# Seven products in two batches instead of five, staging in the plain ones, and W13's stores issued later

## The chip, the core and the metric

The kernel runs on one core of a Trainium2 chip. The metric is the device time of one execution in microseconds; below it is the median of three executions. The engines are TensorE (PE, its weight loads PEld), VectorE (DVE), ScalarE (ACT), GpSimd (POOL) and SyncE (SP), which here only issues DMAs. Each engine takes its instructions in the order of its own queue.

## What is computed

Attention over a packed key set, then two feed-forward blocks, all in float32:

```python
p_packed = sm_attn(p, k, v)               # 8 batches, 8 heads, 32 packed rows, head_dim 64
x = sm_attn(q, p_packed, p_packed)        # 576 rows a batch and head
x = x.transpose(0, 2, 1, 3).reshape(4608, 512)
x2 = (((x @ w1) * (x @ w2)) @ w3) @ w_out     # 512 -> 1024 -> 1024 -> 512
h = x2 @ w_in                                 # 512 -> 2048
out = np.maximum(0.01 * h, h) @ moe2_w_out    # 2048 -> 512
```

## The kernel before

**Numbers.** A float32 operand is used as two parts, hi (rounded) and lo (the remainder), and a product is three matmuls (hi.hi, hi.lo, lo.hi). hi is made on Scalar by a copy, lo on Vector by a subtraction (the helper `sub`, L154). The weights come as 64-bit words; each piece is converted on Scalar (`word`, L293), Vector (`bits`, L299 and L302) and GpSimd (`join`, L309).

**Phase one** goes over eight batches of 576 tokens. `w3 @ w_out` is one matrix, W13, held in four tiles (tags `wr` and `ws`). For a batch there are AT (the second softmax, two tiles) and M (the packed rows times w1 and w2, four tiles); `ab_mm` multiplies them into 16 units of 12 matmuls (a and b for one of 8 feature chunks and one of two token halves of 288), and a times b is the operand of x2. In a *plain* batch (`pieces`, L507) each unit's product is split into hi and lo, and eight units of 24 matmuls make x2 (`x2_unit`). In a batch with *seven products* (`pieces_s`, L776) a times b is kept raw (`ab_raw`), sums of quarters are formed (`x_sum`, L716), each of the seven operands is split (`x_form`, L722 and L154), and seven products of 24 matmuls (`x_product`, L738) take the place of the eight units. The seven matching forms of W13 are made once, in batch 1, from the four quarters (`w13_form`: raw sums on GpSimd, L669; hi and lo), stored to `w13f`, and streamed back in every seven-product batch (`w13_load`). `w13_out` stores W13 itself, to `w13d` (four stores of 1 MB) and, for three of the quarters, to `w13f` (twelve of 256 KB); `w13_back` loads it again for batch 7, which is plain.

**Beside them.** While batch b's pieces run, the attention of batch b+1 is worked in (`attention` in plain batches, `attention_s` in the others): k, q, v loads, scores (`s1_mm`, `s2_mm`), two softmaxes, M's first pair. `pump` and `conv_flush` convert the second block's weights piece by piece. `stage_att(u, a)` stages x2 for phase two: it loads four quarters of 384 columns of one half, forms seven operands (`FORM_B`: 4 sums, 7 hi, 7 lo) and stores them to `xfd`. It borrows the attention's buffers: raw quarters in `v` (5), lo in `PT` (2), hi in `P` (2). One half is staged in each of batches 2 to 6; one more (`stage_b(2, 1)`) in batch 7, the rest in phase two.

**Phase two** (L1013, from 581 us) multiplies the staged operands with forms of w_in and w_out2, also by seven products.

**What sets the order.** The pieces of a batch are numbered slots, 0 to 15 for the units of `ab_mm`, 16 on for x2; tables give the slot at which each further step is written (`slots`, L511). A scheduler then orders each engine's queue by readiness and that order of writing. The prologue and batch 0 have their order written out by hand in `SCRIPT`, on all engines but SP, whose loads and stores the scheduler places. `after(ins, other)` adds an order, not a wait of its own.

Of the kernel before, what the change touches and what calls it, by code (L numbers as in the profile page):

```python
# [55 lines left out]
def tile_kernel(ctx, tc, qT, kT, vL, pT, w12, w3b, wo1, win, wo2, out):  # L56
# [8 lines left out]
    w13d = dram.tile([4, P, 2, 2, 512], F32, name="w13d")  # L65
    w13f = dram.tile([7, P, 2, 2, 512], F32, name="w13f")
# [347 lines left out]
    abh = {}  # L414
    Mp, Mt, abp, ab32, abt, x2p = {}, {}, {}, {}, {}, {}
# [65 lines left out]
    def x2_store(b, th, e):  # L481
        t = main.tile([P, TH], F32, tag="x2s", name="x2s", bufs=6)
        nc.scalar.copy(t, x2p.pop((b, th, e))[:, :TH])  # L483
        nc.scalar.dma_start(out=x2d[:, e, b * S + th * TH:b * S + (th + 1) * TH], in_=t)
# [33 lines left out]
    def attention_s(b):  # L518
        d = {s: [] for s in range(24)}
        d[0] += [lambda: load_v(b, 0)]  # L520
        d[1] += [lambda: load_v(b, 1)]
        d[1] += [lambda: s1_mm(b)]
        for g in range(2):
            d[1] += [lambda g=g: s1_max(b, g)]
            d[2] += [lambda g=g: s1_exp(b, g)]
            d[3] += [lambda g=g: s1_norm(b, g)]
            d[3 + g] += [lambda g=g: load_kq("q", b, g)]
            d[6] += [lambda g=g: t_mm(b, g)]
        for g in range(2):
            d[6] += [lambda g=g: t_copy(b, g)]  # L530
            d[8] += [lambda g=g: pv_mm(b, g)]
        for g in range(2):
            d[8] += [lambda g=g: pv_scale(b, g)]
        d[10] += [lambda: pp_mm(b), lambda: pp_copy(b)]
        d[12] += [lambda: s2_mm(b)]
        for g in range(2):
            s = 12 + 2 * g
# [4 lines left out]
        d[20] += [lambda: m_pair(b, 0)]  # L542
# [3 lines left out]
        return d  # L546

# [67 lines left out]
    def stage(u, a, raw, new, high):  # L615
# [13 lines left out]
        def step(s):  # L629
            form((s,), x, lambda m: high(), lambda m, x: x.bitcast(F32R), lambda m, x: new() if x is None else x, done)  # L630
# [3 lines left out]
    def stage_att(u, a):  # L634
# [4 lines left out]
        return stage(u, a, tile("v", VB), tile("PT", 2), lambda: tile("P", 2)().bitcast(F32R))  # L639
# [7 lines left out]
    def w13_out():  # L647
        for f in range(4):
            nc.sync.dma_start(out=w13d[f], in_=rd(W13[f]))
        for q, m in AQ.items():  # L650
            if m != 7:
                for fa in range(2):
                    for l in range(2):
                        c = int(q[0]) * 256
                        nc.sync.dma_start(
                            out=w13f[m - 1, :, fa, l].rearrange("p (c e) -> p c e", c=2),
                            in_=rd(W13[2 * int(q[1]) + fa])[:, :, l, c:c + 256],
                        )

    def w13_form(fa):  # L660
# [39 lines left out]
    def ab_raw(b, fc, th):  # L700
# [10 lines left out]
        nc.vector.tensor_tensor(out=rawt[b, f][:, th, fc % 2], in0=pb[:, :TH], in1=a, op=ALU.mult)  # L711
# [13 lines left out]
    def x_product(b, m):  # L725
# [18 lines left out]
        for mb in range(2):  # L744
            def new(i, j, tag="x2s", bufs=6):
                t = dsts[b, i, j, mb] = main.tile([P, TH], F32, tag=tag, name="x2s", bufs=bufs)
                nc.scalar.copy(t, ps[mb])

            def add(i, j):
                t = dsts[b, i, j, mb]  # L750
                nc.vector.tensor_tensor(out=t, in0=ps[mb], in1=t, op=ALU.add)
# [27 lines left out]
    def forms_s(b):  # L779
# [6 lines left out]
            14: [lambda: x_sum(b, 6, 5, 3, 5), ],  # L786
            16: [lambda: x_form(b, 6, 0), lambda: x_form(b, 6, 1), lambda: x_sum(b, 7, 7, 3, 7)],
# [19 lines left out]
    FIRST_S, LAST_S = 2, 6  # L807
# [43 lines left out]
    PUMPS = (0, 6, 6, 6, 5, 5, 4)  # L851
    STAGE = {2: (0, 0), 3: (0, 1), 4: (1, 0), 5: (1, 1), 6: (2, 0)}
    for b in range(1, 7):
        staging = {}
        plain = b < FIRST_S
        if plain:
            w13_out()
            staging = spread(w13_form(0) + w13_form(1), 12, 23)
        elif b in STAGE:
            steps = stage_att(*STAGE[b])  # L860
            staging = spread(steps[1:], 11, 19)
            staging[9] = steps[:1]
# [71 lines left out]
    slots(last, fill, spread(stage_b(2, 1), 17, 23))  # L934
# [245 lines left out]
```

## Time and profile before

| | |
|---|---|
| median of three executions | 1293.17 us (1290.62 to 1294.09) |
| profiled execution, its own time | 1288.82 us |
| span from its first to its last instruction | 1287.0 us |
| TensorE busy | 1243.0 us (97%), 8864 matmuls |
| Vector, Scalar, GpSimd busy | 938.5, 624.1, 125.3 us |
| mean granted TensorE clock | 0.995 of full speed |
| moved by DMA | 322.96 MB, mean 251 GB/s |

Batch 0's matmuls begin at 81 us, batch 1's at 152.5, batch 2's at 219, batch 7's at 527.6. A busy TensorE isn't TensorE at its peak: where the span of a batch and its busy time are close, the number of matmuls and their pace set the time; where they differ, a wait does. The row of a waiting instruction names in brackets how long its engine stood idle and whose result released it.

### The profile page before, as it was taken

Reading aid. Unit: us, or ns where it says so; the run is one execution under the profiler, and the core shown is the slowest. Engines: PE = TensorE matmul, PEld = TensorE weight load, DVE = VectorE, ACT = ScalarE, POOL = GpSimd, SP = SyncE. Lnnn points to the kernel's source line nnn. Section 1 sums busy time; section 2 is a strip of 40 time slices with the busy share of each in tenths; the row PEclk is TensorE's granted clock in tenths of the full one; section 3 lists DMA queues with packets and bytes.
Section 4 is the critical chain, followed back from the end, with each engine's and each line's share of the span. In section 5 each row is a group of like instructions: output and inputs, shape, how many; then the busy total and the mean of one; then the engine's idle time right before and its main releaser. Section 6 shows DMA issues by size and latency. Waiting matters only on the chain.

```text
span 1287.0 us, 23438 instructions
## 1 busy us (share of the span) xinstructions
PE 1243.0 (97%) x8864; PEld 1157.4 (90%) x8864; DVE 938.5 (73%) x1524; ACT 624.1 (48%) x1123; POOL 125.3 (10%) x144
## 2 busy tenths in 40 slices
PE   7879998999999999999999999999999999999998
PEld 3339987888888889899999999999999999999998
DVE  7767487888888979666868754886566457786667
ACT  4335353555555556455656554654333344453332
POOL 6444032111110201000000000000000000000000
PEclk9999998999999999999999999999999999999999
DMA  9995138997979795938887778266635764598883
GB/s 368 363 357 180 57 116 296 331 324 239 314 247 306 234 305 175 359 120 280 282 317 283 269 268 289 103 241 249 234 129 190 257 217 167 208 355 299 294 291 124
DMA packets 149986, 322.96 MB, mean 251 GB/s; under 512 B 15856, under 2 KB 71152, under 8 KB 145904
## 3 DMA queue, kind: packets, MB, share of 16 engines
q1 hardware_dynamic: 140656, 312.01, 69.1%
q10 hardware_dynamic: 9216, 9.44, 2.1%
q8 instruction: 70, 1.15, 0.4%
q14 instruction: 44, 0.36, 0.1%
HBM read 230.69 MB, written 90.70 MB: 250 GB/s over the span
## 4 chain that ended last, share of the span: by engine, by line
PE 78%; DVE 12%; DMA 7%; issue 2%; ACT 1%; SPq 1%; POOL 0%; ACTq 0%; DVEq 0%; POOLq 0%
PE b L1013 30%; PE mm L149 16%; PE c L1013 15%; PE a L1013 8%; PE mm L738 3%; PE at L183 3%; DMA c<-w 2%; PE mm L402 1%; DVE v L154 1%; DVE cT L302 1%; DVE abf L154 1%; DMA c<-w3b 1%; DVE abr L716 1%; DVE abr L711 1%; DVE sT L265 1%
## 5 line engine op out<-in xcount | busy, mean ns | idle before, releaser
L149 PEld LDWEIGHTS mm<-AT,M 128*128 128x128 f32 x1536 | 209.9, 191 | 38.1 <-issue 10.2
L149 PE MATMUL mm<-AT,M 128*128 128x288 f32 x1536 | 224.5, 302 | 18.1 <-DVE ab L458 6.0
L1013 PE MATMUL b<-xh,wi 128*128 128x384 f32 x768 | 216.5, 335 | 0.0
L1013 PE MATMUL b<-gh,wo 128*128 128x384 f32 x768 | 215.3, 335 | 0.7 <-DVE o L965 0.7
L1013 PEld LDWEIGHTS b<-gh,wo 128*128 128x128 f32 x768 | 140.4, 188 | 1.0 <-DVE o L965 1.0
L1013 PEld LDWEIGHTS b<-xh,wi 128*128 128x128 f32 x768 | 140.5, 188 | 0.0
L1013 PE MATMUL b<-xl,wi 128*128 128x384 f32 x384 | 128.4, 334 | 0.0
L1013 PE MATMUL b<-gl,wo 128*128 128x384 f32 x384 | 128.3, 334 | 0.0
L738 PEld LDWEIGHTS mm<-abf,W 128*128 128x128 f32 x840 | 112.7, 188 | 11.8 <-DVE abr L711 5.0
L738 PE MATMUL mm<-abf,W 128*128 128x288 f32 x840 | 118.1, 297 | 4.4 <-DVE abr L711 3.8
L609 ACT CAST gh<-gr 128x1152 fp32r<-128x1152 f32 (+1 forms) x72 | 75.7, 1054 | 77.1 <-PE b L1013 48.0
L1013 PE MATMUL c<-gh,wo 128*128 128x384 f32 x384 | 106.4, 334 | 0.0
L1013 PE MATMUL c<-xh,wi 128*128 128x384 f32 x384 | 105.2, 334 | 0.0
L154 DVE TENSOR_TENSOR gl<-gr,gh 128x1152 fp32r<-128x1152 f32 (+1 forms) x72 | 88.0, 1222 | 16.8 <-ACT gh L609 16.7
L965 DVE TENSOR_TENSOR o<-b,o 128x384 f32<-128x384 f32 x108 | 59.5, 555 | 34.3 <-PE b L1013 34.0
L149 PEld LDWEIGHTS mm<-ab,W 128*128 128x128 f32 x576 | 76.4, 188 | 5.0 <-ACT x2s L483 1.7
L149 PE MATMUL mm<-ab,W 128*128 128x288 f32 x576 | 78.1, 295 | 1.5 <-DVE ab L154 1.3
L959 ACT ACTIVATE gr<-gr 128x1152 f32<-128x1152 f32 (+1 forms) x54 | 57.2, 1060 | 44.1 <-DVE gr L965 43.9
L609 ACT CAST gh<-gs 128x1152 fp32r<-128x1152 f32 (+1 forms) x54 | 56.9, 1054 | 44.8 <-PE b L1013 26.5
L973 ACT COPY gr<-b 128x384 f32<-128x384 f32 x96 | 45.6, 479 | 64.9 <-PE b L1013 64.7
L452 ACT COPY a<-mm 128x288 f32<-128x288 f32 x128 | 49.9, 399 | 49.5 <-PE mm L149 40.2
L402 PE MATMUL mm<-ab,w 128*128 128x512 f32 x128 | 59.4, 618 | 13.8 <-POOL ab L309 8.7
(128 smaller groups left out, 2288.4 us busy)
## 6 DMA issues: line engine op xcount, KB each, us to landing
xh<-xfd SPq DMA_DIRECT2D x126, 384.0 KB, 5.6
xl<-xfd SPq DMA_DIRECT2D x126, 384.0 KB, 5.3
W<-w13f SPq DMA_DIRECT2D x23, 1024.0 KB, 7.1
part<-o SPq DMA_DIRECT2D x48, 384.0 KB, 2.5
o<-part SPq DMA_DIRECT2D x48, 384.0 KB, 6.5
xfd<-xt SPq DMA_DIRECT2D x49, 192.0 KB, 2.7
xfd<-xr SPq DMA_DIRECT2D x49, 192.0 KB, 2.6
raw<-kT SPq DMA_DIRECT2D x32, 288.0 KB, 4.7
```

The lines of the kernel that those rows point to most:

```text
L149: ins = nc.tensor.matmul(dst, lhs(i), rhs(j), start=first and n == 0, stop=last and n == 2)
L154: return engine.tensor_tensor(out=out, in0=x, in1=rd(hi), op=ALU.subtract)
L183: ins = nc.tensor.matmul(dst(h)[c * 32:c * 32 + 32], lhs[r, c, :], rhs(c)[r], start=True, stop=True)
L265: nc.vector.tensor_tensor(out=t, in0=t, in1=st[:, :, 0:1].to_broadcast([P, 18, 32]), op=ALU.subtract)
L402: nc.tensor.matmul(w13p[fc], words["3", i][:, c:c + P], words["o", jc], start=w13n[fc] == 1, stop=w13n[fc] == 8)
L452: nc.scalar.copy(a, pa[:, :TH])
L609: gate("a", nc.scalar.copy(hi[step], x[step]))
L738: ins = nc.tensor.matmul(ps[mb], w[:, fa, i, at:at + P], t[:, j, c], start=m in (1, 5, 2) and fa + c + n == 0, stop=m in (4, 3, 2) and fa ...
L959: nc.scalar.activation(out=out, in_=x, func=AF.Prelu, alpha=0.01)
L965: evicted.append(nc.vector.tensor_tensor(**args))
L973: nc.scalar.copy(out, ps)
L1013: ins = nc.tensor.matmul(dst, lhs(l), rhs(r), start=first and n == 0, stop=last and n == total - 1, skip_group_check=True)
```

## The change

- **Fewer seven-product batches.** `FIRST_S` goes from 2 to 5: batches 2, 3 and 4 become plain; only 5 and 6 have seven products.
- **Staging.** Batches 2, 3 and 4 stage two halves each, `(u, 0)` loaded in slot 7 and formed in slots 10 to 14, `(u, 1)` in slots 11 and 15 to 19. Batches 5, 6 and 7 stage none. Each staging sum and lo is ordered behind the latest product, remainder or x2 copy (`latest`, `tied`).
- **W13.** Its stores are sixteen of 256 KB, all to `w13f` (eight places now, `w13d` goes), written in slots 3 to 9 of batch 1 and ordered behind the last v load of batch 2; `w13_back` reads these sixteen blocks. The forms of W13 are made in slots 11 to 19 of batch 1 instead of 12 to 23. In batch 5 the five form loads are written in slots 2 to 9, ordered behind the v loads of batch 6.
- **Attention.** All batches use `attention_s`, whose steps come earlier: first scores at slot 0, transposes at 5, p.v at 7, second scores at 10 (before: 1, 7, 10, 16 in plain batches, 1, 6, 8, 12 in the others).
- `PUMPS` is 6, 5, 5, 5, 6, 5 (before 6, 6, 6, 5, 5, 4), and one `x_sum` is made earlier.

```diff
-    w13d = dram.tile([4, P, 2, 2, 512], F32, name="w13d")
-    w13f = dram.tile([7, P, 2, 2, 512], F32, name="w13f")
+    w13f = dram.tile([8, P, 2, 2, 512], F32, name="w13f")
...
+    def tied(ins):
+        return after(ins, latest[0])
...
     def attention_s(b):
         d = {s: [] for s in range(24)}
-        d[0] += [lambda: load_v(b, 0)]
-        d[1] += [lambda: load_v(b, 1)]
-        d[1] += [lambda: s1_mm(b)]
+        d[0] += [lambda: load_v(b, 0), lambda: load_v(b, 1)]
+        d[0] += [lambda: s1_mm(b)]
...
-        d[12] += [lambda: s2_mm(b)]
+        d[T4] += [lambda: s2_mm(b)]
...
+    T1, T2, T3, T4, MP = 5, 7, 9, 10, 20
...
-    def w13_out():
-        for f in range(4):
-            nc.sync.dma_start(out=w13d[f], in_=rd(W13[f]))
...
+    def w13_blocks(move):
+        for q, m in RAW_AT.items():
+            for fa in range(2):
+                for l in range(2):
+                    c = int(q[0]) * 256
+                    w = rd(W13[2 * int(q[1]) + fa])[:, :, l, c:c + 256]
+                    move(w, w13f[m, :, fa, l].rearrange("p (c e) -> p c e", c=2))
+
+    def w13_out(ahead, n):
+        part = []
+        w13_blocks(lambda w, d: part.append((w, d)))
+        for w, d in part[4 * n:4 * n + 4]:
+            after(nc.sync.dma_start(out=d, in_=w), ahead[0])
...
     def w13_back():
         W13[:] = [w13_tile(f) for f in range(4)]
-        for f in range(4):
-            nc.sync.dma_start(out=rd(W13[f]), in_=w13d[f])
+        w13_blocks(lambda w, d: nc.sync.dma_start(out=w, in_=d))
...
         if b == FIRST_S:
-            d[0] += [lambda m=m: w13_load(m) for m in (1, 5, 6, 3, 2)]
+            for k, m in ((2, 1), (3, 5), (5, 6), (7, 3), (9, 2)):
+                d[k] += [lambda m=m: after_load(w13_load(m), b)]
...
-    FIRST_S, LAST_S = 2, 6
+    FIRST_S, LAST_S = 5, 6
...
-    PUMPS = (0, 6, 6, 6, 5, 5, 4)
-    STAGE = {2: (0, 0), 3: (0, 1), 4: (1, 0), 5: (1, 1), 6: (2, 0)}
+    PUMPS = (0, 6, 5, 5, 5, 6, 5)
+    STAGE = {2: ((0, 0), (0, 1)), 3: ((1, 0), (1, 1)), 4: ((2, 0), (2, 1))}
     for b in range(1, 7):
         staging = {}
-        plain = b < FIRST_S
-        if plain:
-            w13_out()
-            staging = spread(w13_form(0) + w13_form(1), 12, 23)
...
+        if b == 1:
+            staging = spread(w13_form(0) + w13_form(1), 11, 19)
+            for n in range(4):
+                staging.setdefault(3 + 2 * n, []).append(lambda n=n: w13_out([vload[2]], n))
+        for (load, first, last), ua in zip(((7, 10, 14), (11, 15, 19)), STAGE.get(b, ())):
+            steps = stage_att(*ua)
+            staging.setdefault(load, []).append(steps[0])
+            for k, f in spread(steps[1:], first, last).items():
+                staging.setdefault(k, []).extend(f)
...
-    slots(last, fill, spread(stage_b(2, 1), 17, 23))
+    slots(last, fill)
```

**SP in batch 0.** `c<-w` are loads of w12's words (512 KB, three buffers), `w13f<-W` and `w13d<-W` W13's stores, `W<-w13f` the load of a form. Before, word for word:

```order
L690 DMA W_2429<-w13f 128x2048
L334 DMA c_627<-w 128x1024
L334 DMA c_677<-w 128x1024
L655 DMA w13f<-W_81 128x2x256 x2
L649 DMA w13d<-W_81 128x2048
L655 DMA w13f<-W_80 128x2x256
L649 DMA w13d<-W_80 128x2048
L655 DMA w13f<-W_80 128x2x256
L334 DMA c_681<-w 128x1024
L655 DMA w13f<-W_81 128x2x256
L655 DMA w13f<-W_80 128x2x256
L334 DMA c_684<-w 128x1024
```

The same loads in the changed kernel, on to q and the last word of w12:

```order
L335 DMA c_626<-w 128x1024
L335 DMA c_676<-w 128x1024
L335 DMA c_680<-w 128x1024
L335 DMA c_683<-w 128x1024
L335 DMA c_729<-w 128x1024
L335 DMA c_753<-w 128x1024
L168 DMA raw<-qT 128x576 x4
L163 DMA pks_84<-pT 128x128
L335 DMA c_873<-w 128x1024
```

No store stands among them any more. The stores come later, behind the v loads and ahead of batch 2's k:

```order
L175 DMA v<-vL 128x512
L176 DMA v<-vL 64x128
L672 DMA w13f<-W_77 128x2x256 x2
L672 DMA w13f<-W_78 128x2x256 x2
L672 DMA w13f<-W_79 128x2x256 x2
L672 DMA w13f<-W_80 128x2x256 x2
L672 DMA w13f<-W_79 128x2x256 x2
L672 DMA w13f<-W_80 128x2x256 x2
L672 DMA w13f<-W_77 128x2x256 x2
L672 DMA w13f<-W_78 128x2x256 x2
L168 DMA raw<-kT 128x576 x4
```

**Vector in batch 3, ahead of the second softmax** (`sT<-at`). Before, `abr<-mm,a` is a raw product of a seven-product batch, `abr<-abr` a sum for it; `PT<-v`, `v<-v,P` and `PT<-PT,P` are one half's staging:

```order
L711 TENSOR_TENSOR abr<-mm,a 128x288
L716 TENSOR_TENSOR abr<-abr 128x576 x2
L711 TENSOR_TENSOR abr<-mm,a 128x288
L299 TENSOR_SCALAR cT<-c_3488 128x512
L605 TENSOR_TENSOR PT<-v 128x384
L302 SCALAR_TENSOR_TENSOR cT<-c_3488,cT 128x512
L711 TENSOR_TENSOR abr<-mm,a 128x288
L154 TENSOR_TENSOR v<-v,P 128x384
L605 TENSOR_TENSOR PT<-v,PT 128x384
L605 TENSOR_TENSOR v<-v 128x384
L711 TENSOR_TENSOR abr<-mm,a 128x288
L154 TENSOR_TENSOR PT<-PT,P 128x384
```

In the changed kernel, `ab_3716<-mm,a` is a plain batch's product and `ab<-ab_3716,ab` its remainder:

```order
L464 TENSOR_TENSOR ab_3716<-mm,a 128x288
L153 TENSOR_TENSOR ab<-ab_3716,ab 128x288
L613 TENSOR_TENSOR PT<-v 128x384
L153 TENSOR_TENSOR v<-v,P 128x384
L613 TENSOR_TENSOR PT<-v,PT 128x384
L263 STREAM_TRANSPOSE sT<-at 128x576 x2
L265 TENSOR_REDUCE st_3741<-sT 128x18
L464 TENSOR_TENSOR ab_3777<-mm,a 128x288
L265 TENSOR_REDUCE st_3827<-sT 128x18
L266 TENSOR_TENSOR sT<-sT,st_3741 128x576
L300 TENSOR_SCALAR cT<-c_3241 128x512
L464 TENSOR_TENSOR ab_3814<-mm,a 128x288
```

The sums of raw products are gone and each product has its remainder behind it; the first half's staging still begins just ahead of the second softmax, which now stands among the last units of `ab_mm`, and the second half's comes behind it.

## Rows read from the trace of the kernel before

**Rows 1.** Stretches: length, busy us of engines (instructions), granted clock, DMA share, GB/s.

```profile
152.50:215.10 62.60, 61.07 (x605) 55.41 (x603) 48.47 (x81) 27.76 (x64) 16.20 (x15) 1.00 0.54 182
...
219.00:284.30 65.30, 60.92 (x579) 54.20 (x579) 57.94 (x100) 35.02 (x70) 11.88 (x15) 0.95 0.93 326
284.30:346.40 62.10, 59.63 (x579) 52.62 (x579) 52.80 (x99) 33.73 (x68) 9.66 (x12) 1.00 0.84 280
346.40:408.06 61.66, 59.61 (x579) 52.63 (x580) 52.72 (x96) 33.05 (x67) 7.90 (x11) 1.00 0.83 276
408.06:468.73 60.67, 59.24 (x580) 52.68 (x580) 52.75 (x96) 33.16 (x68) 7.94 (x11) 1.00 0.83 274
468.73:527.57 58.84, 58.58 (x582) 52.53 (x580) 50.50 (x93) 33.14 (x67) 5.78 (x4) 1.00 0.68 240
527.57:581.20 53.63, 53.16 (x419) 51.37 (x418) 32.02 (x67) 26.38 (x64) 0.00 (x0) 1.00 0.63 210
...
650.00:1287.00 637.00, 632.28 (x3637) 631.13 (x3635) 431.59 (x642) 291.61 (x458) 0.00 (x0) 1.00 0.68 240
```

**Rows 2.** TensorE's timeline: start, us, instruction, count, idle before and releaser.

```profile
63.33 13.97 PE L402 MATMUL mm<-ab,w 128*128 128x512 f32 x32 [3.10 <-DVE W L154]
...
94.07 6.74 PE L149 MATMUL mm<-AT,M 128*128 128x288 f32 x30 [5.57 <-DVE ab L458]
...
218.97 0.85 PE L149 MATMUL mm<-AT,M 128*128 128x288 f32 x2 [3.89 <-ACT M L426]
222.12 4.62 PE L149 MATMUL mm<-AT,M 128*128 128x288 f32 x22 [2.29 <-DVE M L154]
...
284.54 1.82 PE L149 MATMUL mm<-AT,M 128*128 128x288 f32 x12 [0.47 <-DVE x2s L751]
...
555.83 25.50 PE L149 MATMUL mm<-ab,W 128*128 128x288 f32 x192
```

**Rows 3.** Timelines of Scalar and of Vector, ahead of and in batch 0.

```profile
92.48 0.67 ACT L293 ACTIVATE w<-c 128x512 int32<-128x512 uint32 x1 [8.04 <-DMA c<-w]
...
54.21 0.70 DVE L299 TENSOR_SCALAR ct<-c 128x512 uint32<-128x512 uint32 x1 [4.18 <-DMA c<-w]
...
80.37 1.64 DVE L302 SCALAR_TENSOR_TENSOR cT<-c,cT 128x512 uint32<-128x512 uint32 x1
```

**Rows 4.** Timeline of SP's queue in batch 0.

```profile
77.80 0.94 SPq L655 DMA_DIRECT2D w13f<-W  x2
...
81.96 1.10 SPq L655 DMA_DIRECT2D w13f<-W  x1
83.17 1.10 SPq L334 DMA_DIRECT2D c<-w  x1
```

**Rows 5.** Stretches of batch 0, columns as in rows 1.

```profile
88.50:94.00 5.50, 0.00 (x0) 0.00 (x0) 1.47 (x3) 0.67 (x1) 0.18 (x1) 0.84 1.04 395
94.00:97.00 3.00, 2.84 (x10) 2.49 (x11) 1.06 (x3) 1.72 (x4) 1.13 (x2) 0.50 1.08 392
```

**Rows 6.** DMA issues, 40 to 110 us: count, KB each, median us to landing.

```profile
c<-w SPq DMA_DIRECT2D x13, 512.0 KB, 6.8
w13d<-W SPq DMA_DIRECT2D x4, 1024.0 KB, 8.5
w13f<-W SPq DMA_DIRECT2D x12, 256.0 KB, 7.7
...
c<-win SPq DMA_DIRECT2D x3, 512.0 KB, 4.1
```

**Rows 7.** Timeline of Scalar in batch 1.

```profile
206.90 0.68 ACT L270 ACTIVATE sT<-sT 128x576 f32<-128x576 f32 x1 [5.20 <-DMA w13f<-P]
```

**Rows 8.** Groups of instructions (busy us, mean ns): one staging operation on Vector.

```profile
L154 DVE TENSOR_TENSOR PT<-PT,P 128x384 fp32r<-128x384 f32 (+1 forms) x19 | 11.0, 579 | 0.0
```

**Rows 9.** Timelines of GpSimd and Vector in batch 1.

```profile
189.72 1.46 POOL L669 TENSOR_TENSOR v<-W 128x512 f32<-128x512 f32 x1 [0.61 <-DMA w13f<-v]
...
189.96 1.77 DVE L154 TENSOR_TENSOR v<-v,P 128x512 fp32r<-128x512 f32 x1
```

More of the change, by code (lines that the diff above doesn't have):

```diff
@@ L173, in load_v @@
             src = vL[b, 2 * g + j]
-            nc.sync.dma_start(out=t[:, 0:4], in_=src[0:512].rearrange("(p c) d -> p c d", c=4))
+            vload[b] = nc.sync.dma_start(out=t[:, 0:4], in_=src[0:512].rearrange("(p c) d -> p c d", c=4))
             nc.sync.dma_start(out=t[:64, 4], in_=src[512:576])
@@ L414, in tile_kernel @@
     abh = {}
+    latest = [None]
+    def tied(ins):
+        return after(ins, latest[0])
     Mp, Mt, abp, ab32, abt, x2p = {}, {}, {}, {}, {}, {}
@@ L472, in ab_lo @@
         mark["v"].append(sub(engine, t[:, 1], ab32.pop((fc, th)), t[:, 0]))
+        latest[0] = mark["v"][-1]
     def x2_mm(b, th, e):
@@ L482, in x2_store @@
         t = main.tile([P, TH], F32, tag="x2s", name="x2s", bufs=6)
-        nc.scalar.copy(t, x2p.pop((b, th, e))[:, :TH])
+        latest[0] = nc.scalar.copy(t, x2p.pop((b, th, e))[:, :TH])
         nc.scalar.dma_start(out=x2d[:, e, b * S + th * TH:b * S + (th + 1) * TH], in_=t)
@@ L613, in form, with stage @@
         return {m: (hi[m], lo[m]) for m in hi}
-    def stage(u, a, raw, new, high):
+    def stage(u, a, raw, new, high, tie=False):
         x = {}
@@ L629, in step @@
         def step(s):
-            form((s,), x, lambda m: high(), lambda m, x: x.bitcast(F32R), lambda m, x: new() if x is None else x, done)
+            form(
+                (s,), x, lambda m: high(), lambda m, x: x.bitcast(F32R), lambda m, x: new() if x is None else x, done,
+                {"v": [latest[0]]} if tie else None,
+            )
         return [load] + [lambda s=s: step(s) for s in FORM_B]
@@ L645, in tile_kernel @@
     W_KEPT = (5, 3, 2)
-    def w13_out():
-        for f in range(4):
-            nc.sync.dma_start(out=w13d[f], in_=rd(W13[f]))
[L650 to L658, printed above, removed]
+    RAW_AT = {"00": 0, "01": 1, "11": 3, "10": 7}
+    def w13_blocks(move):
[10 more added lines that the diff above has]
+            after(nc.sync.dma_start(out=d, in_=w), ahead[0])
     def w13_form(fa):
@@ L680, in step @@
                 lambda m, x: (tile("v", VB) if m == 5 else tile("PT", 2)) if x is None else x, done,
+                {"v": [latest[0]]},
             )
@@ L710, in ab_raw @@
         a, pb = abp.pop((fc, th))
-        nc.vector.tensor_tensor(out=rawt[b, f][:, th, fc % 2], in0=pb[:, :TH], in1=a, op=ALU.mult)
+        latest[0] = nc.vector.tensor_tensor(out=rawt[b, f][:, th, fc % 2], in0=pb[:, :TH], in1=a, op=ALU.mult)
     def x_sum(b, m, place, p, q, engine=nc.vector):
@@ L746, in new @@
                 t = dsts[b, i, j, mb] = main.tile([P, TH], F32, tag=tag, name="x2s", bufs=bufs)
-                nc.scalar.copy(t, ps[mb])
+                latest[0] = nc.scalar.copy(t, ps[mb])
             def add(i, j):
                 t = dsts[b, i, j, mb]
-                nc.vector.tensor_tensor(out=t, in0=ps[mb], in1=t, op=ALU.add)
+                latest[0] = nc.vector.tensor_tensor(out=t, in0=ps[mb], in1=t, op=ALU.add)
                 store(i, j)
```

48 lines of the change are left out of this document (23 added, 25 removed).

## The prediction

> **What bounds the kernel now.** I read the table of stretches first: one row a batch, with what each engine did in it [rows 1]. From 650 us on TensorE is busy 632.28 of 637.00 us, and nothing in the change touches that phase; what can move lies before. A plain batch (batch 1) lasts 62.60 us with 61.07 busy; the seven-product batches 3 to 6 last 62.10, 61.66, 60.67 and 58.84 with 59.63, 59.61, 59.24 and 58.58 busy; batch 2 lasts 65.30. So TensorE bounds the batches too, and a seven-product batch saves less than its count says: 24 matmuls of 25.50/192 = 0.133 us [rows 2] are 3.2 us, but batch 3 is only 0.5 us shorter than batch 1. Vector has more to do there (52.80 us against 48.47), and TensorE waits or runs slower beside it.
>
> Then I read TensorE's own timeline for the places where it stood idle [rows 2]: 3.10 us ahead of 63.33, 5.57 ahead of 94.07, 3.89 ahead of 218.97 (between batches 1 and 2) and 2.29 ahead of 222.12. Each was followed back through the engine that released it.
>
> The 5.57 us: Vector and Scalar sit in order behind loads of w12. Scalar waited 8.04 us for one and went on at 92.48 [rows 3]. Vector had freed that load's buffer at 80.37 + 1.64 = 82.01 [rows 3], but SP was issuing W13's stores from 77.80 on, the last of them at 81.96 for 1.10 us, and gave out the load only at 83.17 [rows 4]; it then took 9.3 us. In this stretch the 16 DMA engines are full (share 1.04, 395 GB/s [rows 5]): loads of w12 take 6.8 us to land (median), and among them go 4 stores of 1024 KB, 12 of 256 KB [rows 6] and one early 1024 KB load of a form (the order shows it), 8 MB, some 21 us of the DMA engines at that rate. The next loads, of win, behind the stores, land in 4.1 us [rows 6]. The 3.10 us has the same source: Vector waited 4.18 us for a w12 load before 54.21 [rows 3], and its W13 remainder, which TensorE waits for at 63.33, lies behind that.
>
> The 3.89 and 2.29 us: Scalar waited 5.20 us, up to 206.90, for a store of a W13 form [rows 7]; the exponentials, the new batch's AT and M all stand behind that in order.
>
> **The change, part by part.**
>
> *W13's stores behind v.* Out of the prologue and batch 0 go 7 MB of stores and the 1 MB load. The w12 load can then leave at 82.0 and land 4.1 us later at 86.1, or at 88.8 if it still takes 6.8. Before, TensorE went on 1.6 us after the data (94.07 against 92.48, two conversion operations and a product on Vector), so it would at 87.7 or 90.4. It runs out of work at 88.5: of 5.57 us between 0 and 2.0 are left; I take 0, since the full DMA engines were the cause. The clock comes back with it: it was granted 0.84 in the idle stretch and 0.50 in the three microseconds after it [rows 5], and 30 matmuls took 6.74 us where 30 x 0.133 + 0.2 (allowed for the start of a block) is 4.2: 2.5 us.
> [...]
> At 63.33 up to 3.10 us can go; but TensorE was busy up to 60.23 there, and Scalar's rounding of the same result comes between, so I take 2.0 (bounds 0 and 3.1). What is late next is the conversion itself (Vector, then GpSimd), whose order is as before; I leave 1.0 us for new waits. Sum 5.6 + 2.5 + 2.0 - 1.0 = **9.1 us**, bounds 3.5 and 11.2. Behind the stores stand, on SP, batch 2's k loads: they wait for the scores of batch 1 anyway, and are read only after batch 1 has begun, at 152.5 [rows 1].
>
> *Batches 2, 3, 4 plain.* TensorE gets 24 matmuls more in each. Its busy time should lie between batch 1's 61.07 and batch 6's 58.58 + 3.2 = 61.8; I take 61.4. Vector's work: batch 1's 48.47, minus the 16 operations of W13's forms, plus 2 x 11 of the two halves at 0.58 us [rows 8], 12.7 us; 16 on 512 columns at 0.58 x 512/384 = 0.77 are 12.4, so it stays near 48.8, below batch 6's 50.50, where TensorE idled 0.26 us. Idle time between that and batch 3's 2.47; I take 1.2, near batch 1's 1.53. A batch is then **62.6 us** (bounds 61.1 and 63.9). Against 65.30, 62.10 and 61.66: +2.7, -0.5, -0.9, together **+1.3 us**; the 2.29 idle and the slow clock (22 matmuls in 4.62 us, 1.5 over 22 x 0.133 + 0.2) sit in batch 2's 65.30. The ties put each staging sum behind the latest product, remainder or x2 copy: an order in Vector's queue and no wait of its own.
>
> *Batch 1.* The forms move one slot forward, the second softmax six slots, so the k loads no longer stand in SP's queue ahead of the forms' stores; M is not behind them. The gap of 3.89 us ahead of 218.97 goes: **3.9 us** (bounds 2 and 3.9). The batch itself I leave at 62.6.
>
> *Batches 5 and 6* lose 11 operations, 6.4 us of Vector each; batch 5 takes five form loads of 1 MB, held behind v: 13 us at 395 GB/s, under the half batch (30 us) ahead of the first product that reads them; without that cover they would be a wait there. Batch 5's idle is 60.67 - 59.24 = 1.4: gain 1.5 (0 to 2.1); batch 6: 0.2. *Batch 7* loses one half's staging: 0.3 of its 0.47 us. W13 comes back in 16 pieces of 256 KB from the end of batch 6, some 28 us before x2 of batch 7 reads it: nothing. Together **2.0 us**.
>
> **Sum.** 9.1 + 3.9 + 1.3 + 2.0 = 16.3 us. The profiled execution has 1288.82 us of its own, so it would be 1272.5; the median shown is 1293.17, 4.35 above it, and I take the gain off the median: 1276.9, said as **1277**.
>
> **Rivals.**
> *A, the conversion bounds the prologue.* The loads come early, but Vector, Scalar and GpSimd are no sooner done. For it: the order on these engines is unchanged, and Vector, busy 1.47 us while TensorE stood [rows 5], has the same work to do in less time. Then only 3.5 of the 9.1 us come: 1282.5.
> *B, slower: the two halves' stores block the batch's end.* Hi tiles go through two buffers, each freed only when its store has landed; Scalar, Vector and SP all take things in order, and the x2 copies, AT and M of the next batch stand behind. One such chain cost batch 1 its gap, 3.89 + 2.29 + 1.5 = 7.7 us. Two halves a batch could put it at the ends of batches 2, 3 and 4, and leave it at batch 1's: four times 7.7 against 16.3, 1308. It makes the kernel slower from 16.3/4 = 4.1 us a boundary. Against it: one half a batch was staged in batches 2 to 6, and the longest wait at their ends was the 0.47 us ahead of 284.54 [rows 2]; softmax is now done before the second half starts.
> [...] Vector's remainder of a W13 form took 1.77 us beside a GpSimd sum of 1.46 us [rows 9], ending only after it. The eight sums of W13's forms now fall into the part of batch 1 that also holds softmax; four of them there, each holding Vector up, make 5.8 us: 1282.7. [...] Against it: the same eight ran in batch 1 before, when it lasted 62.60.
> That the change does not do what it says is no rival: SP's order shows the stores behind v.
>
> **How the numbers follow.** Forecast 0.66; A 0.15; C 0.06; plain batches past their bound (over 2.5 us each more, about 1284 or worse) 0.04; B 0.05; better than all bounds 0.04. The range: best, 2.1 more from the stores, 4.5 from batches 2 to 4, 0.6 from batch 5, 1270, and 2.5 for the spread of the runs shown: 1267. Worst, 5.6 less, 3.9 less, 1.5 less: 1288; I end it at 1287. Within 0.3% (3.9 us, about what a measurement of this kernel can tell from no change) lie the tails of A and of slow plain batches: 0.03; slower 0.05, from B; faster 0.92.
>
> **What would show it.** Right: TensorE with no idle time over 1 us between 84 and 216 us and a granted clock of 1.00 there, w12 loads at about 4 us, no gap at the start of batch 2, batches 2 to 4 at 61 to 64 us, and phase two starting some 16 us earlier (before: 581.2). Wrong: the idle time ahead of batch 0's second unit still there (A), idle over 4 us at the starts of batches 3 to 5 (B), or a batch 1 over 66 us (C).

## The result, and the profile after

The changed kernel takes 1277.2 us (median of four executions, 1276.15 to 1277.72), the kernel before 1293.63 us beside it; the ratio is 0.9875, 95% interval [0.9852, 0.9897]. The prediction was 1277.0. The profiled execution took 1276.71 us (span 1274.8, TensorE busy 1246.7, Vector 904.6, Scalar 619.7, GpSimd 127.3 us; 307.21 MB).

The changed kernel by stretches (length, busy us of PE, PEld, DVE, ACT, POOL with instructions, granted clock, DMA share, GB/s): batches 1 to 7, phase two, the stretch of batch 0 in which TensorE had stood, and eight microseconds of batch 2.

```profile
142.22:202.71 60.49, 60.49 (x606) 55.50 (x605) 50.34 (x88) 32.34 (x69) 17.99 (x16) 1.00 0.52 164
202.71:269.82 67.11, 63.84 (x606) 58.18 (x604) 48.64 (x96) 35.03 (x78) 7.33 (x10) 0.95 0.73 248
269.82:333.35 63.53, 61.28 (x605) 55.56 (x604) 47.88 (x97) 34.57 (x77) 9.96 (x12) 1.00 0.75 252
333.35:395.08 61.73, 61.02 (x605) 55.53 (x604) 46.33 (x94) 34.14 (x76) 7.89 (x12) 1.00 0.76 256
395.08:456.02 60.94, 58.58 (x581) 52.46 (x580) 49.98 (x89) 30.79 (x63) 13.24 (x17) 1.00 0.93 341
456.02:513.86 57.84, 57.84 (x579) 52.59 (x580) 46.85 (x84) 29.67 (x60) 6.43 (x5) 1.00 0.55 190
513.86:567.43 53.57, 53.18 (x418) 51.40 (x417) 26.05 (x56) 23.20 (x57) 0.00 (x0) 1.00 0.50 165
567.43:1274.80 707.37, 701.68 (x4034) 700.02 (x4032) 484.12 (x722) 336.11 (x533) 0.00 (x0) 1.00 0.68 241
84.00:97.00 13.00, 13.00 (x182) 10.95 (x183) 11.24 (x25) 8.90 (x23) 7.38 (x10) 1.00 0.81 265
...
208.00:212.00 4.00, 2.10 (x7) 1.75 (x8) 0.31 (x1) 1.34 (x3) 1.42 (x2) 0.67 1.04 355
212.00:216.00 4.00, 4.00 (x18) 4.00 (x18) 2.83 (x9) 2.20 (x7) 0.00 (x0) 0.50 0.98 345
```

Against [rows 1]: batch 1 has no idle time left, batches 3 and 4 are near what was said, and batch 2, at 67.11 us, is longer than before. Its extra sits between about 206 and 216 us: TensorE stood for 2.70 us, and the granted clock was 0.67 over 208 to 212 us and 0.50 over 212 to 216.

TensorE's timeline in the changed kernel answers to [rows 2] (start, us, instruction, count, idle before and releaser): first the prologue and batch 0, then the opening of batch 2.

```profile
41.93 32.03 PE L403 MATMUL mm<-ab,w 128*128 128x512 f32 x74
75.45 1.95 PE L184 MATMUL at<-w,ppT 64*32 64x512 f32 x32 [1.49 <-DVE W L153]
77.75 0.53 PE L148 MATMUL mm<-AT,M 128*128 128x288 f32 x2 [0.35 <-ACT M L432]
79.80 4.64 PE L148 MATMUL mm<-AT,M 128*128 128x288 f32 x22 [1.51 <-DVE M L153]
...
85.50 5.04 PE L148 MATMUL mm<-AT,M 128*128 128x288 f32 x36
...
205.92 1.06 PE L148 MATMUL mm<-AT,M 128*128 128x288 f32 x6 [0.34 <-ACT x2s L490]
209.68 1.81 PE L148 MATMUL mm<-AT,M 128*128 128x288 f32 x6 [2.70 <-ACT x2s L490]
211.71 7.05 PE L148 MATMUL mm<-AT,M 128*128 128x288 f32 x36 [0.22 <-ACT a L458]
```

The 3.10 us ahead of 63.33 and the 5.57 us ahead of 94.07 are gone. SP now gives out W13's stores behind batch 2's v loads (first row, still in batch 0, but after all loads of w12 and the first three of win), and w12's loads land in 4.4 us instead of 6.8 (second row, issues between 40 and 110 us) [rows 4, 6].

```profile
100.75 12.10 SPq L672 DMA_DIRECT2D w13f<-W  x16
```

```profile
c<-w SPq DMA_DIRECT2D x13, 512.0 KB, 4.4
```

Why batch 2 is long is read on Scalar. ACTq rows are DMAs that Scalar issues; a bracket stands on the next row of work.

```profile
201.53 0.41 ACT L490 COPY x2s<-mm 128x288 f32<-128x288 f32 x1
205.10 0.33 ACTq L491 DMA_DIRECT2D x2d<-x2s  x1
205.47 0.40 ACT L490 COPY x2s<-mm 128x288 f32<-128x288 f32 x1 [3.53 <-DMA v<-vL]
208.31 0.33 ACTq L491 DMA_DIRECT2D x2d<-x2s  x1
208.68 0.66 ACT L380 ACTIVATE c<-c 128x512 int32<-128x512 uint32 x1 [2.81 <-DMA v<-vL]
...
211.26 0.40 ACT L458 COPY a<-mm 128x288 f32<-128x288 f32 x1 [1.63 <-DMA w13f<-PT]
```

The copy of x2 was done at 201.94, but its store went out only at 205.10, after a v load that it has nothing to do with had landed. The program's order tells why. In its listing each DMA of SP and of Scalar takes one of eight semaphores, DMAHW0 to DMAHW7, in turn and waits until the DMA that used it last has landed:

```
L491 DMA x2d<-x2s 128x288 [waits DMAHW3_49,Activation_49]
L491 DMA x2d<-x2s 128x288 [waits DMAHW4_49,Activation_49]
```

The trace agrees: the v load issued at 198.20 took 6.8 us to land, and the store that had waited for it left at 205.10. With full DMA engines (share 0.98 to 1.04 over 204 to 216 us) the two stores shown left 3.2 and 2.4 us after their copies, on an engine that also makes the copies, M and a. The same stood in the trace of before, where I had misread it: in [rows 7] sT waited 5.20 us "for a store of a W13 form". The rows ahead of it, and the same once more ahead of AT, in the kernel before:

```profile
201.30 0.40 ACT L483 COPY x2s<-mm 128x288 f32<-128x288 f32 x1 [3.54 <-DMA raw<-kT]
206.53 0.33 ACTq L484 DMA_DIRECT2D x2d<-x2s  x1
...
214.66 0.33 ACTq L484 DMA_DIRECT2D x2d<-x2s  x1
215.03 0.67 ACT L284 CAST AT<-a 128x576 fp32r<-128x576 f32 x1 [4.11 <-DMA c<-win]
```

sT went on right behind the store of 206.53; that store had waited, and the form's store at SP (issued at 199.31, 7.1 us to land) was the DMA whose landing let it go. The next such wait, 4.11 us ahead of AT, is the last ahead of the gap: M's copy stands behind it. In these rows a store's wait stands as idle time of the row behind it: the 5.20 us of the row at 206.90 run from 201.70, the end of the copy, and the store's own row begins only at 206.53.

### The profile page after: what moved, and what is told of

The parts are those of the page before. It is cut to its first block, busy times and chain, and to the rows that moved or that the text cites. A ratio compares the mean times of both kernels' runs of the same rounds, so it can differ in the third digit from the quotient of the medians.

```text
span 1274.8 us, 23459 instructions
## 1 busy us (share of the span) xinstructions
PE 1246.7 (98%) x8936; PEld 1166.8 (92%) x8936; DVE 904.6 (71%) x1488; ACT 619.7 (49%) x1129; POOL 127.3 (10%) x144
## 2 busy tenths in 40 slices
DMA packets 152543, 307.21 MB, mean 241 GB/s; under 512 B 15856, under 2 KB 76272, under 8 KB 151024
## 4 chain that ended last, share of the span: by engine, by line
PE 84%; DMA 9%; DVE 4%; issue 1%; ACT 1%; SPq 0%; POOL 0%; ACTq 0%; DVEq 0%; POOLq 0%
PE b L1031 30%; PE mm L148 21%; PE c L1031 15%; PE a L1031 8%; PE mm L755 3%; PE mm L403 3%; PE at L184 3%; DMA c<-wo 1%; DMA c<-w3b 1%; DMA w13f<-P 1%; DMA xl<-xfd 1%; DMA x2d<-x2s 1%; DMA raw<-qT 1%; DMA xfd<-PT 1%; PE at L241 1%
## 5 line engine op out<-in xcount | busy, mean ns | idle before, releaser
L148 PEld LDWEIGHTS mm<-ab,W 128*128 128x128 f32 x1152 | 153.1, 188 | 5.0 <-ACT x2s L490 4.2
L148 PE MATMUL mm<-ab,W 128*128 128x288 f32 x1152 | 155.5, 295 | 0.0
L1031 PEld LDWEIGHTS b<-xl,wi 128*128 128x128 f32 x384 | 72.1, 188 | 0.4 <-DMA xl<-xfd 0.4
L1031 PEld LDWEIGHTS b<-gl,wo 128*128 128x128 f32 x384 | 72.1, 188 | 0.0
L1031 PEld LDWEIGHTS c<-gh,wo 128*128 128x128 f32 x384 | 70.2, 188 | 0.0
L1031 PEld LDWEIGHTS c<-xh,wi 128*128 128x128 f32 x384 | 70.0, 188 | 0.0
```

What stands on the lines that cost most here:

```text
L148: ins = nc.tensor.matmul(dst, lhs(i), rhs(j), start=first and n == 0, stop=last and n == 2)
L1031: ins = nc.tensor.matmul(dst, lhs(l), rhs(r), start=first and n == 0, stop=last and n == total - 1, skip_group_check=True)
```

## The experiments

Medians are of four executions each, but for the last one, a single execution. Where a batch's length is given it is from the profiled execution.

**Only the stores moved.** In the kernel before, the sixteen stores go to slots 3 to 9 of batch 1, behind v:

```diff
-            w13_out()
             staging = spread(w13_form(0) + w13_form(1), 12, 23)
+            for n in range(4):
+                staging.setdefault(3 + 2 * n, []).append(lambda n=n: w13_out(n))
...
```

> The kernel before with one part of the change alone: W13's sixteen stores (the same 7 MB, four of 1 MB and twelve of 256 KB) are written in slots 3, 5, 7 and 9 of batch 1 and ordered behind the v load of batch 2, instead of at batch 1's head, from where they ran in the prologue and batch 0. Theory (the stores filled the DMA engines ahead of the w12 loads): the idle times of 3.10 us ahead of 63.33 and of 5.57 us ahead of 94.07 go, batch 1 begins 9 to 10 us earlier than 152.5, and the whole is 9 to 10 us shorter, about 1284. Rival A (the conversion bounds the prologue): 3.5 us, about 1290. Rival D (the 7 MB only move: in batch 1 they stand in the way of v, q and k loads and of the form loads of batch 2): batch 1 begins 10 us earlier, but batches 1 and 2 together are 3 to 8 us longer, so that 2 to 7 us are left, 1287 to 1292.

Measured 1280.55 us, ratio 0.9907 [0.9875, 0.9938]. Batch 1 began at 140.78 (152.49 before), and batches 1 and 2 together took 130.4 us against 132.1: rivals A and D fall, though batch 3 is 2.1 us longer, waiting 2.12 for a form's load. This one part brings 13.4 us, more than the 9 to 10 expected (its profiled execution is 9.0 below the first trace of before and 15.0 below the second); the whole change, in its own comparison, 16.4.

**Only the stores put back,** in the changed kernel:

```diff
+            w13_out()
             staging = spread(w13_form(0) + w13_form(1), 11, 19)
-            for n in range(4):
-                staging.setdefault(3 + 2 * n, []).append(lambda n=n: w13_out([vload[2]], n))
...
```

> The changed kernel with one part undone: the sixteen stores of W13 are written at batch 1's head again, with nothing ahead of them, all else as changed. Theory: batch 1 begins 9 to 10 us later than 142.2 and the whole is about 9.5 us longer, some 1287; batch 1 itself, without 4 MB in it, is no shorter than 60 us, since TensorE bounds it (60.49 with no idle time). Rival (the new places of attention and of the forms carry the gain of the prologue): less than 3 us longer.

Measured 1285.86 us, 8.7 longer, as expected; batch 1 began at 147.90 and lasted 60.47. In batch 0 TensorE stood again:

```profile
91.23 4.05 PE L148 MATMUL mm<-AT,M 128*128 128x288 f32 x17 [2.88 <-ACT a L458]
```

Batch 1 begins only 5.7 us later, not 9 to 10. Two differences are on record: the stores are 4 MB here, not 7 with a load of 1, and the changed kernel's 142.2 holds 1.5 us of slow clock (last section). Batch 2 and phase two are 1.6 and 1.7 longer as well. The rest of the change alone, the smaller stores and the missing early load included, brings 8.1 us (1293.99 to 1285.86). The two parts overlap: 13.4 and 8.1 are more than 16.4.

**x2's stores on GpSimd,** in the changed kernel from batch 1 on:

```diff
-        nc.scalar.dma_start(out=x2d[...], in_=t)
+        queue = nc.gpsimd if b else nc.scalar
+        queue.dma_start(out=x2d[...], in_=t)
```

> The changed kernel with Scalar's stores of x2 (eight a plain batch) issued by GpSimd from batch 1 on. Theory L (a store that Scalar issues has to wait until an earlier DMA that shares its semaphore has landed, and with full DMA engines at the end of a batch this holds the x2 copies, exponentials and a of the next batch behind it: 205.92, 209.68 and 211.71 are TensorE's idle times of 0.34, 2.70 and 0.22 us at batch 2's start, and its clock is 0.50 to 0.67 over 208 to 216): the waits of 3.5, 2.8 and 4.0 us on Scalar go, batch 2 goes from 67.1 to 62.5 to 64 us, batches 3 and 5 lose about 1.5 us each, together 5 to 7 us, about 1271. Rival M (the data are late: v's loads and the DMA engines' full share set the time, whoever issues): batch 2 stays at 66 to 67 us and the whole within 1.5 us of 1277. Rival N (GpSimd's issue is slow or stands behind its own conversions and holds the six x2s buffers): 2 to 10 us longer, with x2 copies that wait for a store.

Measured 1273.93 us: 3.3 less than the changed kernel, where 5 to 7 were expected. Batch 2 fell from 67.11 to 62.16 us, as theory L had it, and Scalar's waits there went. But batches 4 and 5 became 1.7 and 1.1 us longer. (Of the 4.0 us between the two traces, 1.2 are the clock of batch 0, see the last section.) Scalar, in the opening of batch 4:

```profile
332.84 0.74 ACT L209 ACTIVATE P<-at,st 128x576 f32<-128x576 f32 x1 [1.88 <-issue]
...
335.26 0.74 ACT L209 ACTIVATE P<-at,st 128x576 f32<-128x576 f32 x1 [1.59 <-DMA xfd<-P]
```

The second exponential waits for the store of a staged hi tile whose buffer it takes over: the wait that rival B named, with Scalar's own out of its way. TensorE stood 2.38 us behind it.

**x2's stores on GpSimd in batch 1 alone** (`if b == 1`).

> The changed kernel with x2's stores on GpSimd in batch 1 alone; all other batches issue them from Scalar. Theory L (the opening of batch 2 is set by Scalar's own stores of x2, which wait for an earlier DMA to land): batch 2 is 62 to 63 us as with all of them on GpSimd (62.16; 67.11 as changed), batch 3 stays at 62.6 to 63.5, batches 4 and 5 are back at 61.7 and 60.9 (63.45 and 62.03 with all on GpSimd); the whole 1271 to 1273. Rival (the gain lay in the later batches, or the longer batches 4 and 5 come from the start of batch 2): batch 2 over 65 us, or batches 4 and 5 still over 125 us together.

Measured 1273.99 us; batch 2 took 62.71. Batches 4 and 5 did not come back (65.20 and 61.45): at batch 4's opening the last store of x2, from a copy that ended at 330.03, left at 334.40. This profiled execution was the slowest of the four (1271.78 to 1276.47), so its later batches may be longer than usual. L holds for batch 2, and the later openings pay in one place or another.

**The same in the kernel before** (batches 1 and 7 store through this step).

> The kernel before with the stores of x2 issued by GpSimd in batches 1 and 7, the two that store through this step besides batch 0. Theory L (the gap between batches 1 and 2, 3.89 us ahead of 218.97 and 2.29 ahead of 222.12, comes from Scalar's own x2 stores, which wait for an earlier DMA to land): both go down to under 1.5 us together and the whole is 4 to 6 us shorter, 1288 to 1290. The prediction's reading (Scalar waits for the stores of W13's forms, whose hi tiles must be free for the next ones, and these are issued by SP as before): the gap stays at 4 us or more and the whole within 1.5 us of before.

TensorE at the boundary of batches 1 and 2:

```profile
216.23 0.53 PE L149 MATMUL mm<-AT,M 128*128 128x288 f32 x2 [1.21 <-ACT M L426]
218.26 4.02 PE L149 MATMUL mm<-AT,M 128*128 128x288 f32 x17 [1.50 <-DVE M L154]
```

6.18 us of idle time [rows 2] became 2.71; neither reading said that (under 1.5, or 4 and more). The kernel before itself has 4.87 (2.29 and 2.58) in its second trace below, so by these traces Scalar's own store accounts for 2.2 to 3.5 us of the gap, and not for all of it. What is left has the prediction's wait in it, on Scalar:

```profile
202.88 0.69 ACT L270 ACTIVATE sT<-sT 128x576 f32<-128x576 f32 x1 [3.90 <-DVE sT L265]
207.15 0.62 ACT L610 CAST P<-v 128x512 fp32r<-128x512 f32 x1 [3.59 <-DMA w13f<-P]
207.67 0.68 ACT L270 ACTIVATE sT<-sT 128x576 f32<-128x576 f32 x1
...
212.28 0.67 ACT L284 CAST AT<-a 128x576 fp32r<-128x576 f32 x1 [2.25 <-DVE a L279]
```

A hi tile of a W13 form waited for the store of an earlier one, up to 207.15, and the softmax's second half went on only behind it, 0.4 us earlier than in the kernel before (208.08). What went is the wait ahead of AT: 212.28 here, 215.03 before. The whole became slower, 1297.24 against 1292.68 us, with batch 5 at 62.91 and phase two at 709.7 us; why these pay stays open, and the time therefore does not bear L out, only the gap does, in part.

**The old attention beside batch 1,** in the changed kernel (`attention` in place of `attention_s` where `b == 1`).

> The changed kernel with the attention of batch 2 at its old slots while batch 1 runs (first scores at slot 1, second scores at 16 with their softmax up to 21, k loads at 17 and 19); the forms of W13 stay in slots 11 to 19. The prediction's reading (the gap of 3.9 us between batches 1 and 2 goes because softmax and forms come earlier): the gap comes back, batches 1 and 2 last 131 to 134 us against 127.6, the whole 1280 to 1284. Theory L (the waits of Scalar's stores of x2 set the place; they only moved from M to the a of batch 2): batches 1 and 2 stay within 1.5 us of 127.6, with an idle time of 2 us or more ahead of M at the batch's head in place of that ahead of 209.68.

Measured 1277.74 us, no difference. Batches 1 and 2 took 62.00 + 64.13 = 126.1 us (127.6 as changed), with an idle time ahead of M instead:

```profile
204.35 0.53 PE L148 MATMUL mm<-AT,M 128*128 128x288 f32 x2 [1.49 <-ACT M L432]
```

Two more, of 0.72 and 0.73 us, follow it; theory L had said 2 us or more ahead of M. So the earlier softmax is worth nothing as a time: with it waits of much the same length (2.94 us in all here, 3.26 as changed) fall on x2 and a instead of M.

**One half a batch,** in the changed kernel:

```diff
-    STAGE = {2: ((0, 0), (0, 1)), 3: ((1, 0), (1, 1)), 4: ((2, 0), (2, 1))}
+    STAGE = {2: ((0, 0),), 3: ((0, 1),), 4: ((1, 0),), 5: ((1, 1),), 6: ((2, 0),)}
...
```

> The changed kernel with staging as before the change: one half in each of batches 2 to 6 (loaded in slot 9, formed in slots 11 to 19) and one in batch 7. Theory (a second half costs a plain batch little, since TensorE bounds it; a half in a seven-product batch costs 1.5 us in batch 5, 0.2 in 6, 0.3 in 7): batches 2 to 4 become 0 to 1 us shorter each, batches 5 to 7 together 2 us longer; the whole within 1.5 us of 1277. Rival B (two halves' stores block the ends of the batches): batches 3 and 4 and the start of 5 become 2 us or more shorter each, and the whole is 1271 to 1273. The opposite (a half costs a seven-product batch more than 3 us): 1282 or more.

Measured 1286.49 us, the opposite of rival B in sum, and both at once in detail: with seven products in batches 5 and 6, two halves in the plain batches are worth 9.3 us. Batches 3 and 4 fell to 60.49 us each (63.53 and 61.73 with two halves); batches 5 and 6 rose to 66.35 and 65.31. TensorE and, ahead of it, Scalar at the boundary of 5 and 6:

```profile
455.61 2.77 PE L148 MATMUL mm<-AT,M 128*128 128x288 f32 x10 [4.75 <-ACT x2s L764]
```

```profile
454.23 0.88 ACTq L773 DMA_DIRECT2D x2d<-x2s  x2
455.15 0.70 ACT L764 COPY x2s<-mm 128x288 f32<-128x288 f32 x2 [4.98 <-DMA v<-vL]
```

Again a store of x2 from Scalar. With the new slots, ties and pumps a half costs these batches 5.4 and 7.5 us; before, with one half each, they took 60.67 and 58.84 [rows 1].

**No seven products at all,** from the changed kernel with one half a batch: `FIRST_S` past the last batch, and

```diff
-        if b == 1:
-            staging = spread(w13_form(0) + w13_form(1), 11, 19)
-            for n in range(4):
-                staging.setdefault(3 + 2 * n, []).append(lambda n=n: w13_out([vload[2]], n))
...
-    w13_back()
```

> The changed kernel without seven products at all: every batch is plain, W13 stays where it is, so its sixteen stores, its forms, their stores and all form loads go; one half is staged in each of batches 2 to 6 and one in batch 7. Theory P (a plain batch with one half lasts 60.49 us, as batches 3 and 4 did with one half each; seven products bring 24 matmuls, 3.2 us, less in a batch and give it all back in waits and in batch 2's opening): batches 1 to 6 are 60.5 us each, 363 against 371.6 as changed, the whole 1268 to 1270. Rival S (seven products pay): batches 5 and 6 lose 0 and 2.7 us and batch 2 gains less than 2: the whole at 1277 or above.

Measured **1265.36 us**, ratio 0.9793 [0.9778, 0.9808], four executions within 0.9 us. Batches 1 to 6 are 60.48 to 60.54 us each, with no idle time. Two of them, columns as above:

```profile
202.85:263.39 60.54, 60.54 (x605) 55.55 (x604) 41.14 (x83) 31.16 (x69) 7.86 (x11) 1.00 0.65 215
...
444.86:505.34 60.48, 60.48 (x606) 55.49 (x604) 42.25 (x83) 31.07 (x69) 7.22 (x5) 1.00 0.46 157
```

This beats both kernels. Seven products save 24 matmuls a batch, but over batches 1 to 6 the changed kernel spends 371.6 us where this one spends 363.0.

**The kernel before without seven products,** its own attention and pumps kept.

> The kernel before (its own slots of attention, its own pumps) without seven products: all batches plain, W13 never leaves, one half staged in each of batches 2 to 6 and one in batch 7. Theory P (with W13's traffic gone no wait is left at a batch's end, so where attention stands does not matter): batches 1 to 6 are 60.5 to 61 us each and the whole 1265 to 1268. Rival (the earlier softmax is needed all the same): idle times of 1 us and more in the batches, 62 to 63 us each, the whole 1272 to 1282.

Measured 1264.72 us, ratio 0.9787 [0.9763, 0.9811]; batches 1 to 6 at 60.33 to 60.35 but for batch 5 (61.92). Without W13's traffic and with one half a batch, where attention stands makes no difference.

**No seven products, two halves in batches 2 to 4.**

> The kernel without seven products (all batches plain, W13 never leaves), but with two halves staged in each of batches 2, 3 and 4 and none in 5 to 7, as in the changed kernel. With one half each every batch lasted 60.5 us and the whole 1265.4. Theory B' (the second half itself fills the DMA engines at a batch's end, and Scalar's x2 stores wait): batches 2 to 4 are 1 to 3 us longer each, batches 5 and 6 are 60.5, the whole 1268 to 1273. Rival (only W13's traffic ahead of them did that, and two halves cost nothing by themselves): all batches 60.5 and the whole within 1.5 us of 1265.4. This also says how the 12 us between the changed kernel and the one without seven products split into staging and W13.

Measured 1274.46 us, 9.1 above one half a batch. The batches behind the doubled ones, 3 to 5, took 63.41, 62.39 and 61.98 us; phase two, 707.2 against 705.8. Scalar at the head of batch 3:

```profile
263.63 0.40 ACT L490 COPY x2s<-mm 128x288 f32<-128x288 f32 x1 [0.40 <-PE mm L148]
268.00 0.33 ACTq L491 DMA_DIRECT2D x2d<-x2s  x1
268.37 0.40 ACT L458 COPY a<-mm 128x288 f32<-128x288 f32 x1 [4.34 <-PE mm L148]
```

Theory B': the store of a copy that ended at 264.03 left at 268.00, and the next batch's a behind it. (The row's releaser, a matmul, had long been done; it is the store that ended last.) The DMA engines were not quite full there, share 0.82 over 263 to 268 us. On this way, the 11.8 us between the changed kernel and the one without seven products and with one half split into 9.1 for the second half and 2.7 for W13 and the seven products. The split depends on the way: with seven products the second half saved 9.3 us, without them it costs 9.1, so with one half a batch the seven products cost 21.1.

**The same with x2's stores of batches 2 to 4 on GpSimd.**

> The kernel without seven products and with two halves in batches 2 to 4 (its batches 3 to 5: 63.41, 62.39, 61.98 us, the whole 1274.5), with x2's stores of batches 2 to 4 issued by GpSimd instead of Scalar. Theory L (the second half costs time because Scalar's last store of x2 in a batch waits, 4 us in the trace, for an earlier DMA to land, and the first a of the next batch stands behind it): batches 3 to 5 are 60.5 to 61.5 us each, the whole 1268 to 1270. Rival B'' (the exponentials of the next batch wait for the stores of staged hi tiles, whose buffers they take over, whoever issues x2's stores, as at 335.26 with all stores on GpSimd): batches 3 to 5 stay at 186 us or more together, the whole within 2 us of 1274.5.

Measured 1269.75 us (1267.93 to 1273.5), within what L said; batches 3 and 4 are not, at 62.55 and 64.91. The profiled execution was the slowest of the four: its batch 4 has rival B'' in it, and TensorE stood 2.75 us behind the wait.

```profile
334.99 0.74 ACT L209 ACTIVATE P<-at,st 128x576 f32<-128x576 f32 x1 [1.97 <-DMA xfd<-P]
```

Two waits thus stand in line at a batch's opening, Scalar's store of x2 and the staged tiles' stores that hold P's buffers; taking the first away shows the second.

**The kernel before again,** unchanged.

> The kernel before once more, for a second trace: its profiled execution took 1288.82 us, while the seven timed ones lie between 1290.58 and 1296.48. Theory V (the stretches whose DMA engines are full differ between executions): most of a difference of 2 to 6 us is found in the prologue and batch 0 (71.12 us from 81.37 to 152.49 in the first trace) and in batch 1 to 2, and the batches 3 to 6 and phase two agree within 0.5 us. Rival (an even slowdown, by the clock or the start): each stage is longer by the same share, 0.2 to 0.4%.

This execution took 1294.75 us, 5.9 above the first trace. 3.2 of it are in batch 2 and 1.2 ahead of batch 0's start; batch 1 was 1.6 shorter, batches 3 to 7 and phase two 3.1 longer together. Batch 2 there (columns as above):

```profile
218.63:287.41 68.78, 61.61 (x579) 54.92 (x580) 58.34 (x101) 34.94 (x70) 11.86 (x15) 0.95 0.90 311
```

Theory V holds for batch 2, not for batch 0; and batch 3 (0.8) and phase two (0.7) did not agree within 0.5 us. The first trace was a short execution, so the difference of the traces understates the gain: 12.1 us from it, 18.0 from this one, 16.4 between the medians.

## Why the prediction was right, and where it was not

| stretch | before, two traces | after | change | predicted |
|---|---|---|---|---|
| up to batch 1 | 152.5, 153.7 | 142.2 | -10.3, -11.5 | -9.1 |
| batch 1 and the gap | 66.5, 64.9 | 60.5 | -6.0, -4.4 | -3.9 |
| batch 2 | 65.6, 68.8 | 67.1 | +1.5, -1.7 | -2.7 |
| batches 3, 4 | 123.5, 124.2 | 125.3 | +1.7, +1.1 | +1.4 |
| batches 5 to 7 | 173.1, 174.8 | 172.3 | -0.8, -2.5 | -2.0 |
| phase two | 705.8, 706.6 | 707.4 | +1.6, +0.8 | 0 |

(Lengths between the first matmuls of the batches; batch 2 and the gap are cut as in the prediction's sum.) The total was right, and its largest term for the right reason. Two other terms were wrong with opposite signs, so the sum is better than its parts, and its closeness, 0.2 us, is luck: the two traces of before alone lie 5.9 apart. Of the signs named, w12's loads (4.4 us) and the end of both idle times in the prologue came; idle time and clock up to 216 us, batch 2 and phase two (13.7 us earlier than in the first trace, not 16) did not. The worst end of the range leaves out the 1.9 us between the gap's two bounds; with them it would be 1290, and nothing hangs on it here.

- **W13's stores** (9.1): right, a little small. Both idle times and the slow clock behind them went, 5.57 + 3.10 + 2.5. The 1.0 us left for new waits came as clock: the 22 matmuls at 79.80 took 4.64 us, not 3.17. What the prediction had wrong is where the stores went: not into batch 1 but into the middle of batch 0 (from 100.75 us on), where nothing waited for them.
- **The gap** (3.9) and **batches 2 to 4** (62.6 each): the failed step is the reading of [rows 7]. At 206.90 Scalar was held by its own store of x2 waiting its turn; the wait for a form's hi tile that the prediction named ends nearly as late (207.15 with x2's stores on GpSimd), but the last wait ahead of M, 4.11 us, is again a store of x2. That wait came with full or nearly full DMA engines at the batch's end (shares of 0.82 to 1.04), and not only with a late softmax. So the gap did not go: it turned from 3.89 us ahead of M into 2.70 ahead of 209.68 and a slow clock, within batch 2, which became 67.11 instead of 62.6. The old attention in batch 1 costs nothing, and stores on GpSimd bring 4.95 us there.
- **Batch 1** (62.6) was over-estimated: without idle time it is 60.49. I had kept the 1.5 us of batch 1 of before as the way of plain batches; every plain batch without such a wait takes 60.3 to 60.6.
- **Two halves** (nothing beyond the wait allowed): rival B was given 0.05, at 7.7 us a boundary. As a time it was wrong; without seven products a loss was there behind every doubled batch, 1.5 to 2.9 us in the trace, 9.1 us by the medians in all. What held the openings first was Scalar's own store of x2; B's mechanism, the hi tiles, came behind it. That one half had been staged without a wait said little about two.
- **Batches 5 to 7** (2.0): 0.8 or 2.5 by the trace of before that one takes; too near to their difference to judge. Batch 5, given 1.5 of it, took 60.94 us with 2.4 idle, against 60.67 and 61.05, so its part did not show.
- **Rivals A and C** (C: GpSimd's sums hold Vector up, and TensorE behind it): TensorE doesn't pause between 84 and 204 us (120.00 us busy of 120.00), so neither the conversion nor GpSimd's sums in batch 1 hold it. Vector did take longer beside a sum, in the changed kernel 1.78 us for the remainder at 185.83, beside the sum at 185.75, against 0.68 for the one at 182.56 with none beside it.
- **Phase two** was 0.8 to 1.6 us longer with the same work. The waits of TensorE that the profile names there are 2.2 us, against 1.4 and 1.8 in the two traces of before: a part; the rest stays open.
- **The base.** The profiled execution of before was 4.35 us below its median; taking the gain off the median was the right choice, as the second trace shows.

## What to carry to other kernels

In these programs a DMA that Scalar issued held Scalar up while the DMA that had last used its semaphore had not landed: the stores of x2 named above left 2.4 to 4.8 us after their copies. Where the DMA engines are busy at a stage's end (shares of 0.82 to 1.04 here), try issuing from an idle engine (3.3 us gained in the changed kernel, 4.6 lost in the one before) or thin the traffic there, and look for the store ahead of the row that shows the idle time. A cheaper algorithm that must stream operands is to be priced with its traffic: 24 matmuls a batch were worth less than the waits that W13's forms and the crowded staging brought. And where removing a wait leaves the stage as long, ask what stood second in line before counting the gain.

## What was not expected of the hardware

The same three pauses of TensorE ahead of batch 0 (1.49, 0.35 and 1.51 us) were followed by a lower clock in four of the ten changed or derived kernels' traces that have them, and by a full one in the others: 4.6 us or 3.2 for the same 22 matmuls. The granted clock was 0.62 to 0.64 on the mean in the slow ones, and 1.00 in the others. The changed kernel, and the one with stores on GpSimd in batch 1:

```profile
79.80:84.40 4.60, 4.60 (x26) 4.44 (x27) 4.46 (x6) 2.07 (x5) 1.82 (x3) 0.64 0.61 194
```

```profile
79.86:84.40 4.54, 4.54 (x56) 3.74 (x57) 4.47 (x7) 1.95 (x4) 1.76 (x3) 1.00 0.64 194
```

The two programs differ only in who issues the stores of batch 1, behind these rows. So about 1.5 us can come or go with no difference in the program up to there. What decides between the two clocks is not shown; no run here moved the pauses. Where the rest of the scatter comes from is not shown either: the changed kernel without seven products and with one half lies within 0.9 us, the kernel before within 3.6 in the same comparison, but the kernel before without seven products, as free of waits but for one batch, within 3.4.
